# A decode step of cached attention: V of a unit in one load into a buffer of its own, K in three buffers

## The chip, the cores and the metric

The kernel runs on one core of one Trainium2 chip. The metric is the device time of one execution in microseconds, the median of three runs. The span that a profile shows goes from the first to the last instruction of one profiled execution, and is a little shorter than that execution's own time.

## The reference

Two batches with one new token each, width 512. A is attention of 32 query heads over a cache of 8 key/value heads, 32768 positions and a head width of 128; B is a small gated network on the same normalised input. The output is `x + A * silu(B)`.

```python
x = A_x                                    # [2, 1, 512]
xn = _layernorm(x, axis=-1)
# A: q = xn @ wq, 32 heads; k, v: [2, 8, 32768, 128], 4 query heads share one
scores = einsum("bhqd,bhkd->bhqk", q, k) * (128 ** -0.5)
p = softmax(scores)
s = einsum("bhqk,bhkd->bhqd", p, v).reshape(2, 1, 4096) @ wo
# B: h = gelu(layernorm(xn) @ w1), shifted by one or two tokens, @ w2; with one
#    token every shift leaves zeros, so x1 = xn
h2 = gelu(layernorm(x1) @ w3) @ w4
g = silu(x1 + h2)
return x + s * g
```

All tensors are bf16. K and V of the cache have 134 MB each; they are read once, and with the weights 280.5 MB come from HBM.

## The kernel before, in words

The attention is cut into 16 **units**, one for each batch and key/value head (`units`, `NU` = 16). A unit has 8 MB of K and 8 MB of V. Before the change both come in two **chunks** (`NCH` = 2) of 4 MB: a chunk lies in SBUF as 128 partitions with 32 KB each, and is read from HBM as 128 contiguous rows of 32 KB.

A chunk of K is worked on by `k_job`: DVE transposes it in four blocks (`transposed`, one instruction for 2048 words of 4 bytes per partition, into one of `KTB` = 2 buffers `ktb`), and PE makes scores from each block with 8 matmuls (`scores`, into the PSUM tile `sc`). `waiting` is a list of blocks whose scores are still to be issued; `flush(keep)` issues those beyond `keep`, and PE so runs one block behind DVE. When the last scores of a unit are issued, `softmax_front` has DVE take a maximum; the rest of the softmax is two pieces of work (`step1`, `step2`) that are put on the list `glue` and issued one at a time between other work. They end with `pT`, the transposed probabilities.

A chunk of V is worked on by `v_job`: 32 matmuls of four 32-column strips of PE, with 16 columns of `pT` as weights and 512 columns of V, add to the PSUM tile `acc`. After the second chunk `unit_end` copies `acc` and puts the normalisation on `glue`.

`loads` is the one list of all loads, and also the order in which the jobs are issued: the first chunk of K, wq, the second chunk of K, w3, w4, and then for each unit n, chunk by chunk, K of unit n + 1 and V of unit n; last wo. All loads are DMAs on SP's queue, into one pool of `SLOTS` = 5 buffers with 32 KB per partition (`issue`). Load i + 5 is issued in the program after job i; on the chip its DMA waits on SP until the buffer that it takes has been read. The last chunk of V comes in two halves, and wo in four pieces, so that their matmuls can start as each piece lands.

```python
    for n in range(NU):
        for c in range(NCH):
            if n + 1 < NU:
                loads.append(("K", n + 1, c))
            loads.append(("V", n, c))
```

In `v_job` the scores that still wait (`flush(0)`) are issued after the first four matmuls of a chunk, so the scores of the last K block and the value products alternate on PE. The engines follow the order of the program each by itself; the order is written out by hand.

`mlp_job` (network B) stands where w4 stands in `loads`; `q_job` makes the queries within the first chunk of K; `o_final` and `wo_job` make the output from the 16 units.

In the profile L110 is the DMA of K and V, L116 that of wo, L286 the transposes of K, L234 the scores, L313 the value products, L335 the copy of `acc`, L427 the last products of network B, and L365 those of `wo_job`.

Of the kernel before, what the change touches and what calls it, by code (L numbers as in the profile page):

```python
# [9 lines left out]
BF16 = mybir.dt.bfloat16  # L10
# [4 lines left out]

UT = 128
GT = 16
SLOTS = 5
KTB = 2
KG = 2  # L20
LAG = 1
# [3 lines left out]
def kernel(  # L25
# [14 lines left out]
    nc = tc.nc  # L40

    B, Sq, D = A_x.shape
    _, Hkv, Sk, Dh = A_k_cache.shape
    HD = A_wq.shape[1]
    Hq = HD // Dh
    rep = Hq // Hkv
    Fdim = B_w3.shape[1]
    assert Sq == 1 and B == 2 and Dh == 128 and rep == 4 and D == 512 and Fdim % 128 == 0
    DK = D // 128
    FK = Fdim // 128  # L50
    CH = UT * 128
    NCH = Sk // CH
    NB = UT // GT
    NS = 32 // rep
# [8 lines left out]
    NU = len(units)  # L63

    ctx.enter_context(tc.manual_schedule())
    head = ctx.enter_context(tc.tile_pool(name="head", bufs=1))
    slots = ctx.enter_context(tc.tile_pool(name="slots", bufs=SLOTS))
    pers = ctx.enter_context(tc.tile_pool(name="pers", bufs=1))
    kt_pool = ctx.enter_context(tc.tile_pool(name="ktb", bufs=KTB))
    p_pool = ctx.enter_context(tc.tile_pool(name="prob", bufs=2))  # L70
# [12 lines left out]
    NR = HD // 128  # L83
    wo_v = A_wo.rearrange("(p r) d -> p (r d)", r=NR)

    loads = [("K", 0, 0), ("wq",)]
    loads += [("K", 0, c) for c in range(1, NCH)]
    loads += [("w3",), ("w4",)]
    for n in range(NU):
        for c in range(NCH):  # L90
            if n + 1 < NU:
                loads.append(("K", n + 1, c))
            loads.append(("V", n, c))
    wo_cuts = [0, NR // 2, 3 * NR // 4, NR - 4, NR]
    loads += [("wo",)]
    tiles = {}

    def issue(i):
        if i >= len(loads):
            return  # L100
        what = loads[i]
        t = slots.tile([128, UT * Dh], BF16, tag="slot", name=f"slot_{what[0]}")
        if what[0] in ("K", "V"):
            b, g = units[what[1]]
            c = what[2]
            src = A_k_cache if what[0] == "K" else A_v_cache
            sv = src[b, g, c * CH:(c + 1) * CH, :].rearrange("(p t) d -> p (t d)", p=128)
            w = UT * Dh // 2 if what == ("V", NU - 1, NCH - 1) else UT * Dh
            for w0 in range(0, UT * Dh, w):
                nc.sync.dma_start(out=t[:, w0:w0 + w], in_=sv[:, w0:w0 + w])  # L110
        elif what[0] == "wq":
            nc.sync.dma_start(
                out=t[:, 0:DK * HD].rearrange("p (k f) -> p k f", k=DK), in_=wq_v)
        elif what[0] == "wo":
            for r0, r1 in zip(wo_cuts, wo_cuts[1:]):
                nc.sync.dma_start(out=t[:, r0 * D:r1 * D], in_=wo_v[:, r0 * D:r1 * D])  # L116
        elif what[0] == "w3":
            nc.sync.dma_start(
                out=t[:, 0:DK * Fdim].rearrange("p (k f) -> p k f", k=DK), in_=w3_v)
        else:  # L120
            nc.sync.dma_start(
                out=t[:, 0:FK * D].rearrange("p (f d) -> p f d", f=FK), in_=w4_v)
        tiles[what] = t

    issue(0)
    x_bf = tmp.tile([B, D], BF16, tag="row", name="x_bf")
    nc.scalar.dma_start(out=x_bf[:, :], in_=A_x[:, 0, :])
    x4 = pers.tile([128, 128], BF16)
    nc.gpsimd.memset(x4[:, :], 0.0)
    for b in range(B):  # L130
        nc.scalar.dma_start(out=x4[b:128:32, :], in_=A_x[b, 0, :].rearrange("(j c) -> j c", j=4))
    for i in range(1, SLOTS):
        issue(i)


    ident = head.tile([128, 128], BF16)
# [79 lines left out]
    glue = []  # L216
# [73 lines left out]
    def flush(keep):  # L290
        while len(waiting) > keep:
            scores(*waiting.pop(0))
# [10 lines left out]
            if glue:  # L303
                glue.pop(0)()

    def v_job(n, c):
        vv = tiles[("V", n, c)][:, :].rearrange("p (e i t d) -> p e t i d", i=4, t=GT, d=Dh)
        for e in range(NB // 4):
            half, r0 = (c * NB + e * 4) // NS, (c * NB + e * 4) % NS * rep
            pT = unit_st[n]["pT"]  # L310
            for t in range(GT):
                j = t % 4
                nc.tensor.matmul(  # L313
                    acc[32 * j:32 * j + 16, :].rearrange("p (i d) -> p i d", d=Dh),
                    lhsT=pT[:, half * GT + t, r0:r0 + 16],
                    rhs=vv[:, e, t, :, :],
                    start=(c == 0 and e == 0 and t < 4),
                    stop=(c == NCH - 1 and e == NB // 4 - 1 and t >= GT - 4),
                    tile_position=(0, 32 * j),
                )  # L320
                if e == 0 and t == 3:
                    flush(0)
                elif t % 4 == 3 and glue and n == NU - 1:
                    glue.pop(0)()
        if c == NCH - 1:
            unit_end(n)

    s_ps = s_psp.tile([128, 128], F32)
    nc.vector.memset(s_ps[:, :], 0.0)
# [1 line left out]
    def unit_end(n):  # L331
        b, g = units[n]
        st = unit_st.pop(n)
        acs = tmp.tile([128, 4 * Dh], F32, tag="row", name="acs")
        nc.vector.tensor_copy(out=acs[:, :], in_=acc[:, :])  # L335

        def step1():
            ot = mi_psp.tile([128, 2 * rep], F32, tag="mi", name="ot")
            nc.tensor.matmul(ot[:, rep:2 * rep], lhsT=ones_f[:, :], rhs=st["Sm"][:, :], start=True, stop=True)  # L339
            for i in range(4):  # L340
                nc.tensor.matmul(  # L341
                    ot[:, 0:rep], lhsT=acs[:, i * Dh:(i + 1) * Dh], rhs=sel[:, i, :],
                    start=(i == 0), stop=(i == 3))
            rc = sm_pool.tile([128, rep], F32, tag="rc", name="rc")
            nc.vector.reciprocal(out=rc[:, :], in_=ot[:, rep:2 * rep])  # L345
            nc.vector.tensor_tensor(
                out=oQ[:, b, g * rep:(g + 1) * rep], in0=ot[:, 0:rep], in1=rc[:, :], op=ALU.mult)

        glue.append(step1)
# [49 lines left out]
                out=qz[32 * i:32 * i + 32, n % 2, :, c0:c0 + rep], in_=qp[32 * i:32 * i + 32, :, b, g, :])  # L399

    def mlp_job():
        w3 = tiles[("w3",)][:, 0:DK * Fdim].rearrange("p (k q f) -> p k f q", k=DK, f=FK)
        w4 = tiles[("w4",)][:, 0:FK * D].rearrange("p (f d) -> p f d", f=FK)
        hT_ps = mi_psp.tile([128, FK * B], F32, tag="mi", name="hT")
        for f in range(FK):
            for k in range(DK):
                nc.tensor.matmul(  # L407
                    hT_ps[:, f * B:(f + 1) * B],
                    lhsT=w3[:, k, f, :],
                    rhs=xT[:, DK + k, :],  # L410
                    start=(k == 0), stop=(k == DK - 1),
                )
        hf = pers.tile([128, FK * B], F32)
        nc.vector.tensor_copy(out=hf[:, :], in_=hT_ps[:, :])
        x2 = pers.tile([128, FK * B], F32)
        nc.vector.tensor_mul(out=x2[:, :], in0=hf[:, :], in1=hf[:, :])
        nc.vector.tensor_scalar(out=x2[:, :], in0=x2[:, :], scalar1=0.044715, scalar2=1.0, op0=ALU.mult, op1=ALU.add)
        inner = pers.tile([128, FK * B], F32)
        nc.vector.tensor_mul(out=inner[:, :], in0=hf[:, :], in1=x2[:, :])
        th = pers.tile([128, FK * B], F32)  # L420
        nc.scalar.activation(out=th[:, :], in_=inner[:, :], func=ACT.Tanh, scale=GELU_C)
        nc.vector.tensor_scalar(out=th[:, :], in0=th[:, :], scalar1=0.5, scalar2=0.5, op0=ALU.mult, op1=ALU.add)
        h_bf = pers.tile([128, FK * B], BF16)
        nc.vector.tensor_mul(out=h_bf[:, :], in0=hf[:, :], in1=th[:, :])  # L424
        h2_ps = mi_psp.tile([B, D], F32, tag="mi", name="h2")
        for f in range(FK):
            nc.tensor.matmul(  # L427
                h2_ps[0:B, :],
                lhsT=h_bf[:, f * B:(f + 1) * B],
                rhs=w4[:, f, :],  # L430
                start=(f == 0), stop=(f == FK - 1),
            )
        t_f = tmp.tile([B, D], F32, tag="row", name="t_f")
        nc.vector.tensor_add(out=t_f[:, :], in0=xn[:, :], in1=h2_ps[0:B, :])
        sig = tmp.tile([B, D], F32, tag="row", name="sig")
        nc.scalar.activation(out=sig[:, :], in_=t_f[:, :], func=ACT.Sigmoid)
        nc.vector.tensor_mul(out=g_sb[:, :], in0=t_f[:, :], in1=sig[:, :])
        for b in range(B):
            nc.scalar.dma_start(
                out=g4[b:128:32, :], in_=g_sb[b:b + 1, :].rearrange("b (j c) -> b j c", j=4))  # L440


    for i, what in enumerate(loads):
        if what[0] == "K":
            k_job(what[1], what[2])
        elif what[0] == "V":
            if what[2] == 0:
                while glue and unit_st[what[1]]["pT"] is None:
                    glue.pop(0)()
            v_job(what[1], what[2])  # L450
        elif what == ("w4",):
            mlp_job()
        elif what[0] == "wo":
            while glue:
                glue.pop(0)()
            o_final()
            wo_job()
        issue(i + SLOTS)

    sg = tmp.tile([128, 128], F32, tag="row", name="sg")  # L460
    nc.vector.tensor_tensor(out=sg[:, :], in0=s_ps[:, :], in1=g4[:, :], op=ALU.mult)
# [34 lines left out]
```

## Time and profile before

| | |
|---|---|
| median of 3 runs | 660.98 us (660.77 to 661.1) |
| the profiled execution | 660.7 us, its span 658.9 us |
| mean granted TensorE clock | 0.818 |
| busy: PE, weight loads, DVE, ACT | 420.9, 173.8, 365.4, 38.5 us |
| DMA | 280.88 MB, mean 426 GB/s over the span |
| one transpose of K (L286, 128 of them) | 2298 ns |
| K loads (32 of 4096 KB): issue to landing | 39.9 us, median |
| V loads (31 of 4096 KB): issue to landing | 34.3 us, median |

Instructions are told by line, engine, operation and tile; "x28" says that 28 of them are merged. A time in brackets is how long the engine stood idle before, and what ended that. A DMA's line on SPq tells when it was issued, not when its bytes moved. In slices a digit is the busy share in tenths. In stretches each engine has its busy time and number of instructions, and the last three columns are the granted clock of TensorE, the busy share of the 16 DMA engines and GB/s; a DMA packet is booked at one point of time, so that a very short stretch can show a share over 1.

### The profile page before, as it was taken

The page shows a single profiled execution, that of the slowest core. Times are in us where ns is not written, and L with a number is a line of the kernel's source. Part 1 is how long each engine was busy: PE and PEld are TensorE (multiplying, and loading weights), DVE is VectorE, ACT ScalarE, POOL GpSimd, SP SyncE. Part 2 cuts the span into 40 slices and gives each one's busy share as a digit, 9 for nine tenths or more (in the row PEclk, how much of TensorE's full clock was granted, in tenths as well). Part 3 has the DMA queues.
Part 4 walks back from the last instruction along what each step waited for, and adds up shares of the span by engine and source line. Part 5 has one row for each costly group of instructions (what it writes and reads, how often), then busy time and mean ns, then how long its engine had stood idle before and what let it go on. Part 6 is the DMA issues. An engine that isn't in the chain of part 4 may idle for free.

```text
span 658.9 us, 5935 instructions
## 1 busy us (share of the span) xinstructions
PE 420.9 (64%) x2595; PEld 173.8 (26%) x2595; DVE 365.4 (55%) x312; ACT 38.5 (6%) x104; POOL 2.2 (0%) x10
## 2 busy tenths in 40 slices
PE   0587767477575657746567784657668565764775
PEld 0342223132221223222122332223222222322233
DVE  6174856556654645655555654555565455465531
ACT  1103010000000000000000000000000100000000
POOL 1000000000000000000000000000000000000000
PEclk9997877987786898777898686888868688887776
DMA  9999999999999999999999999999999999999995
GB/s 382 420 438 441 417 444 433 426 443 420 442 431 430 439 426 437 432 427 442 427 436 429 430 443 424 437 432 430 443 422 437 432 431 438 425 436 437 430 425 246
DMA packets 10445, 280.88 MB, mean 426 GB/s; under 512 B 1194, under 2 KB 1204, under 8 KB 1460
## 3 DMA queue, kind: packets, MB, share of 16 engines
q1 hardware_dynamic: 10376, 280.50, 98.8%
q8 instruction: 20, 0.33, 0.2%
q14 instruction: 5, 0.04, 0.0%
q10 hardware_dynamic: 44, 0.01, 0.0%
HBM read 280.50 MB, written 0.00 MB: 426 GB/s over the span
## 4 chain that ended last, share of the span: by engine, by line
DMA 71%; PE 17%; DVE 9%; issue 1%; ACT 1%; SPq 0%; DVEq 0%; ACTq 0%
DMA slot_K<-in_A_k_cache_dram 62%; PE sc L234 12%; DVE ktb L286 7%; DMA slot_wo<-in_A_wo_dram 6%; DMA slot_wq<-in_A_wq_dram 3%; PE acc L313 3%; DVE pT L275 1%; ACT pr L271 1%; PE h L427 1%; PE qT L374 1%; PE hT L407 1%; PE bc L264 0%; DVE nb L268 0%; ACT qz L398 0%; DVE Sm L278 0%
## 5 line engine op out<-in xcount | busy, mean ns | idle before, releaser
L234 PE MATMUL sc<-ktb,qz 128*128 128x512 bf16 x1024 | 310.9, 460 | 198.4 <-DVE ktb L286 196.7
L286 DVE STREAM_TRANSPOSE ktb<-slot_K 128x2048 uint32<-128x2048 uint32 x128 | 292.1, 2298 | 169.9 <-DMA slot_K<-in_A_k_cache_dram 142.3
L234 PEld LDWEIGHTS <-qz 128*128 128x128 bf16 x1024 | 110.7, 112 | 369.0 <-issue 305.6
L313 PE MATMUL acc<-slot_V,pT 128*16 128x512 bf16 x1024 | 70.8, 399 | 5.4 <-DMA slot_V<-in_A_v_cache_dram 5.4
L313 PEld LDWEIGHTS <-pT 128*16 128x16 bf16 x1024 | 23.2, 90 | 54.9 <-issue 34.6
L248 DVE TENSOR_REDUCE m<-sc 128x1 f32<-128x1024 f32 x16 | 19.5, 1221 | 29.8 <-PE sc L234 29.8
L398 ACT COPY qz<-qp 32x16 bf16<-32x16 bf16 x64 | 12.9, 201 | 330.0 <-PE sc L234 308.3
L275 DVE STREAM_TRANSPOSE pT<-pr 128x1024 bf16<-128x1024 bf16 x16 | 19.9, 1245 | 21.2 <-ACT pr L271 21.2
L271 ACT ACTIVATE pr<-sc,nb 128x1024 bf16<-128x1024 f32 x16 | 17.8, 1113 | 234.1 <-DVE nb L268 234.1
L335 DVE COPY acs<-acc 128x512 f32<-128x512 f32 x16 | 11.1, 692 | 14.1 <-PE acc L313 14.1
L341 PE MATMUL ot<-sel,acs 128*128 128x4 f32 x128 | 18.2, 265 | 0.3 <-DVE acs L335 0.3
L341 PEld LDWEIGHTS ot<-sel,acs 128*128 128x128 f32 x128 | 17.2, 209 | 0.4 <-DVE acs L335 0.4
L268 DVE TENSOR_SCALAR nb<-bc 128x1 f32<-128x1 f32 x16 | 2.5, 158 | 22.4 <-PE bc L264 22.4
L374 PE MATMUL qT<-xT,slot_wq 128*128 128x2 bf16 x128 | 3.6, 165 | 12.1 <-DMA slot_wq<-in_A_wq_dram 12.1
L264 PEld LDWEIGHTS bc<-ones_f,gx 1*128 1x128 f32 x32 | 6.5, 250 | 12.9 <-issue 10.9
L264 PE MATMUL bc<-ones_f,gx 1*128 1x1 f32 x32 | 7.8, 311 | 1.0 <-DVE gx L258 1.0
L339 PEld LDWEIGHTS ot<-Sm,ones_f 128*128 128x128 f32 x32 | 6.2, 203 | 3.8 <-issue 1.7
L253 PE MATMUL mT<-identf,m 128*1 128x128 f32 x16 | 4.4, 276 | 3.6 <-DVE m L248 3.6
L374 PEld LDWEIGHTS <-slot_wq 128*128 128x128 bf16 x128 | 3.5, 104 | 12.2 <-DMA slot_wq<-in_A_wq_dram 12.2
L427 PE MATMUL h<-slot_w,h_bf 128*2 128x512 bf16 x14 | 4.9, 525 | 1.6 <-DVE h_bf L424 1.6
L345 DVE RECIPROCAL rc<-ot 128x4 f32<-128x4 f32 x16 | 2.4, 149 | 5.5 <-PE ot L341 5.5
L200 PE MATMUL treg<-ident,xn_bf 2*128 2x2 bf16 x4 | 0.3, 174 | 7.8 <-DVE xn_bf L188 7.8
(70 smaller groups left out, 62.4 us busy)
## 6 DMA issues: line engine op xcount, KB each, us to landing
slot_K<-in_A_k_cache_dram SPq DMA_DIRECT2D x32, 4096.0 KB, 39.9
slot_V<-in_A_v_cache_dram SPq DMA_DIRECT2D x31, 4096.0 KB, 34.3
slot_wq<-in_A_wq_dram SPq DMA_DIRECT2D x1, 4096.0 KB, 21.4
slot_V<-in_A_v_cache_dram SPq DMA_DIRECT2D x2, 2048.0 KB, 29.5
slot_w<-in_B_w_dram SPq DMA_DIRECT2D x2, 1792.0 KB, 39.0
slot_wo<-in_A_wo_dram SPq DMA_DIRECT2D x1, 2048.0 KB
slot_wo<-in_A_wo_dram SPq DMA_DIRECT2D x1, 1024.0 KB
slot_wo<-in_A_wo_dram SPq DMA_DIRECT2D x2, 512.0 KB, 38.7
```

The lines of the kernel that those rows point to most:

```text
L234: nc.tensor.matmul(sc[:, half, :].rearrange("p (t k) -> p t k", k=32), lhsT=qz[:, n % 2, k, off:off + 128], rhs=kv[:, k // 2, k % 2, :, :] ...
L248: nc.vector.tensor_reduce(out=m1[:, :], in_=st["sc"][:, :, :].rearrange("p x k -> p (x k)"), axis=AX.X, op=ALU.max)
L264: nc.tensor.matmul(bc[:, :], lhsT=st["gx"][:, :, :].rearrange("o x h -> o (x h)"), rhs=ones_f[0:1, 0:1], start=True, stop=True)
L271: nc.scalar.activation(out=pr[:, :], in_=st["sc"][:, :, :].rearrange("p x k -> p (x k)"), func=ACT.Exp, bias=nb[:, 0:1], scale=inv_sqrt_dh ...
L275: nc.vector.transpose(out=pT[:, :, :].rearrange("p t r -> p (t r)"), in_=pr[:, :])
L286: nc.vector.transpose(out=ktb[:, :], in_=kw)
L313: nc.tensor.matmul(acc[32 * j:32 * j + 16, :].rearrange("p (i d) -> p i d", d=Dh), lhsT=pT[:, half * GT + t, r0:r0 + 16], rhs=vv[:, e, t, ...
L335: nc.vector.tensor_copy(out=acs[:, :], in_=acc[:, :])
L341: nc.tensor.matmul(ot[:, 0:rep], lhsT=acs[:, i * Dh:(i + 1) * Dh], rhs=sel[:, i, :], start=(i == 0), stop=(i == 3))
L374: nc.tensor.matmul(qT_ps[:, h * B:(h + 1) * B], lhsT=w[:, k * HD + h * Dh:k * HD + (h + 1) * Dh], rhs=xT[:, k, :], start=(k == 0), stop=(k ...
L398: nc.scalar.copy(out=qz[32 * i:32 * i + 32, n % 2, :, c0:c0 + rep], in_=qp[32 * i:32 * i + 32, :, b, g, :])
L427: nc.tensor.matmul(h2_ps[0:B, :], lhsT=h_bf[:, f * B:(f + 1) * B], rhs=w4[:, f, :], start=(f == 0), stop=(f == FK - 1),)
```

## The change

K and V no longer share buffers. K keeps chunks of 4 MB and has a pool of `KSLOTS` = 3 buffers with 32 KB per partition; wo takes one of them at the end. V has one buffer with 64 KB per partition (`vslot`), and a unit's V is loaded into it by one DMA of 8 MB. Only the last unit's V is cut into three pieces, of 4, 2 and 2 MB. At the start this buffer holds wq, w3 and w4 side by side.

A partition now holds 64 KB that lie together in HBM, for K as for V. Rows of a V load are so 64 KB long. Rows of a K load keep 32 KB, and lie 64 KB apart.

In the order of loads and jobs both chunks of K of unit n + 1 come before V of unit n. Ahead of V's job all waiting scores and everything on `glue` are issued, and then the 64 value products of the unit in one go. A load is now issued in the program once the job has been issued that frees its buffer (`ready`, `issue_ready`), still in the order of the list.

```diff
-SLOTS = 5
+KSLOTS = 3
...
-    slots = ctx.enter_context(tc.tile_pool(name="slots", bufs=SLOTS))
+    slots = ctx.enter_context(tc.tile_pool(name="slots", bufs=KSLOTS))
+    vslot = ctx.enter_context(tc.tile_pool(name="vslot", bufs=1))
...
+    W3, W4 = DK * HD, DK * HD + DK * Fdim
     loads = [("K", 0, 0), ("wq",)]
     loads += [("K", 0, c) for c in range(1, NCH)]
     loads += [("w3",), ("w4",)]
     for n in range(NU):
-        for c in range(NCH):
-            if n + 1 < NU:
-                loads.append(("K", n + 1, c))
-            loads.append(("V", n, c))
+        if n + 1 < NU:
+            loads += [("K", n + 1, c) for c in range(NCH)]
+        loads.append(("V", n))
...
+    kload = [w for w in loads if w[0] in ("K", "wo")]
+    done = set()
+
+    def ready(what):
+        if what[0] in ("K", "wo"):
+            j = kload.index(what)
+            return j < KSLOTS or kload[j - KSLOTS] in done
+        if what[0] == "V":
+            return ("V", what[1] - 1) in done if what[1] else ("w4",) in done
+        return True
+
+    def issue_ready():
+        while loads and ready(loads[0]):
+            issue(loads.pop(0))
+
+    def issue(what):
+        if what[0] in ("K", "wo"):
+            t = slots.tile([128, UT * Dh], BF16, tag="slot", name=f"slot_{what[0]}")
+        elif what[0] in ("wq", "V"):
+            t = vslot.tile([128, NCH * UT * Dh], BF16, tag="v", name=f"slot_{what[0]}")
+        else:
+            t = tiles[("wq",)]
...
-            sv = src[b, g, c * CH:(c + 1) * CH, :].rearrange("(p t) d -> p (t d)", p=128)
-            w = UT * Dh // 2 if what == ("V", NU - 1, NCH - 1) else UT * Dh
-            for w0 in range(0, UT * Dh, w):
-                nc.sync.dma_start(out=t[:, w0:w0 + w], in_=sv[:, w0:w0 + w])
+            sv = src[b, g, :, :].rearrange("(p t) d -> p (t d)", p=128)
+            if what[0] == "K":
+                nc.sync.dma_start(out=t[:, :], in_=sv[:, what[2] * UT * Dh:(what[2] + 1) * UT * Dh])
+            else:
+                cuts = [0, NCH * UT * Dh]
+                if what[1] == NU - 1:
+                    cuts = [0, UT * Dh, UT * Dh * 3 // 2, NCH * UT * Dh]
+                for w0, w1 in zip(cuts, cuts[1:]):
+                    nc.sync.dma_start(out=t[:, w0:w1], in_=sv[:, w0:w1])
...
-    def v_job(n, c):
-        vv = tiles[("V", n, c)][:, :].rearrange("p (e i t d) -> p e t i d", i=4, t=GT, d=Dh)
-        for e in range(NB // 4):
-            half, r0 = (c * NB + e * 4) // NS, (c * NB + e * 4) % NS * rep
+    def v_job(n):
+        vv = tiles[("V", n)][:, :].rearrange("p (x i t d) -> p x t i d", i=4, t=GT, d=Dh)
+        nx = NCH * NB // 4
+        for x in range(nx):
+            half, r0 = x * 4 // NS, x * 4 % NS * rep
...
-                if e == 0 and t == 3:
-                    flush(0)
-                elif t % 4 == 3 and glue and n == NU - 1:
-                    glue.pop(0)()
-        if c == NCH - 1:
-            unit_end(n)
+        unit_end(n)
...
-    for i, what in enumerate(loads):
+    for what in order:
         if what[0] == "K":
             k_job(what[1], what[2])
         elif what[0] == "V":
-            if what[2] == 0:
-                while glue and unit_st[what[1]]["pT"] is None:
-                    glue.pop(0)()
-            v_job(what[1], what[2])
+            flush(0)
+            while glue:
+                glue.pop(0)()
+            v_job(what[1])
...
-        issue(i + SLOTS)
+        done.add(what)
+        issue_ready()
```

More of the change, by code (lines that the diff above doesn't have):

```diff
@@ L96 @@
     tiles = {}
[L98 to L102, printed above, removed]
+    kload = [w for w in loads if w[0] in ("K", "wo")]
[17 more added lines that the diff above has]
+            t = tiles[("wq",)]
         if what[0] in ("K", "V"):
             b, g = units[what[1]]
-            c = what[2]
             src = A_k_cache if what[0] == "K" else A_v_cache
-            sv = src[b, g, c * CH:(c + 1) * CH, :].rearrange("(p t) d -> p (t d)", p=128)
-            w = UT * Dh // 2 if what == ("V", NU - 1, NCH - 1) else UT * Dh
-            for w0 in range(0, UT * Dh, w):
-                nc.sync.dma_start(out=t[:, w0:w0 + w], in_=sv[:, w0:w0 + w])
+            sv = src[b, g, :, :].rearrange("(p t) d -> p (t d)", p=128)
[7 more added lines that the diff above has]
+                    nc.sync.dma_start(out=t[:, w0:w1], in_=sv[:, w0:w1])
         elif what[0] == "wq":
@@ L118, in issue @@
             nc.sync.dma_start(
-                out=t[:, 0:DK * Fdim].rearrange("p (k f) -> p k f", k=DK), in_=w3_v)
+                out=t[:, W3:W3 + DK * Fdim].rearrange("p (k f) -> p k f", k=DK), in_=w3_v)
         else:
             nc.sync.dma_start(
-                out=t[:, 0:FK * D].rearrange("p (f d) -> p f d", f=FK), in_=w4_v)
+                out=t[:, W4:W4 + FK * D].rearrange("p (f d) -> p f d", f=FK), in_=w4_v)
         tiles[what] = t
-    issue(0)
+    order = list(loads)
+    issue(loads.pop(0))
     x_bf = tmp.tile([B, D], BF16, tag="row", name="x_bf")
@@ L131 @@
         nc.scalar.dma_start(out=x4[b:128:32, :], in_=A_x[b, 0, :].rearrange("(j c) -> j c", j=4))
-    for i in range(1, SLOTS):
-        issue(i)
+    issue_ready()
     ident = head.tile([128, 128], BF16)
@@ L315, in v_job @@
                     lhsT=pT[:, half * GT + t, r0:r0 + 16],
-                    rhs=vv[:, e, t, :, :],
-                    start=(c == 0 and e == 0 and t < 4),
-                    stop=(c == NCH - 1 and e == NB // 4 - 1 and t >= GT - 4),
+                    rhs=vv[:, x, t, :, :],
+                    start=(x == 0 and t < 4), stop=(x == nx - 1 and t >= GT - 4),
                     tile_position=(0, 32 * j),
                 )
-                if e == 0 and t == 3:
-                    flush(0)
-                elif t % 4 == 3 and glue and n == NU - 1:
-                    glue.pop(0)()
-        if c == NCH - 1:
-            unit_end(n)
+        unit_end(n)
     s_ps = s_psp.tile([128, 128], F32)
@@ L401, in mlp_job @@
     def mlp_job():
-        w3 = tiles[("w3",)][:, 0:DK * Fdim].rearrange("p (k q f) -> p k f q", k=DK, f=FK)
-        w4 = tiles[("w4",)][:, 0:FK * D].rearrange("p (f d) -> p f d", f=FK)
+        w3 = tiles[("w3",)][:, W3:W3 + DK * Fdim].rearrange("p (k q f) -> p k f q", k=DK, f=FK)
+        w4 = tiles[("w4",)][:, W4:W4 + FK * D].rearrange("p (f d) -> p f d", f=FK)
         hT_ps = mi_psp.tile([128, FK * B], F32, tag="mi", name="hT")
@@ L457 @@
             wo_job()
-        issue(i + SLOTS)
+        done.add(what)
+        issue_ready()
     sg = tmp.tile([128, 128], F32, tag="row", name="sg")
```

## The prediction

> **What bounds the kernel now.** I read the page first, by its slices and its queues.
>
> ```profile
> PE   0587767477575657746567784657668565764775
> DVE  6174856556654645655555654555565455465531
> DMA  9999999999999999999999999999999999999995
> q1 hardware_dynamic: 10376, 280.50, 98.8%
> ```
>
> PE and DVE are half to three quarters busy, the DMA engines all the time but for the ends. So the next view is the table of stretches, taken over 12 loads of the middle, over the last V halves, and over the edges of the run:
>
> ```profile
> core 0: us, PE busy (x) PEld busy (x) DVE busy (x) ACT busy (x) POOL busy (x), PEclk, DMA share, GB/s
> 109.38:225.55 116.17, 75.33 (x423) 30.03 (x423) 66.26 (x51) 6.03 (x18) 0.00 (x0) 0.81 1.00 432
> 636.00:648.00 12.00, 9.68 (x77) 4.64 (x69) 1.03 (x3) 0.00 (x0) 0.00 (x0) 0.50 1.01 429
> ...
> 3.40:3.60 0.20, 0.00 (x0) 0.00 (x0) 0.20 (x2) 0.20 (x1) 0.00 (x0) 1.00 0.00 0
> 3.60:3.80 0.20, 0.00 (x0) 0.00 (x0) 0.20 (x2) 0.20 (x1) 0.00 (x0) 1.00 3.07 1311
> 4.80:5.00 0.20, 0.00 (x0) 0.00 (x0) 0.20 (x2) 0.00 (x0) 0.00 (x0) 1.00 2.65 1147
> 654.00:654.50 0.50, 0.32 (x13) 0.13 (x5) 0.00 (x0) 0.00 (x0) 0.00 (x0) 0.50 0.16 66
> 654.50:655.00 0.50, 0.03 (x4) 0.03 (x7) 0.00 (x0) 0.00 (x0) 0.00 (x0) 0.76 0.00 0
> ```
>
> The last three columns count: granted PE clock, DMA share, GB/s. The middle has share 1.00 at 432 GB/s; a 4 MB load passes every 116.17 / 12 = 9.68 us. The kernel is one stream of 280.5 MB that never stops. Its time is the stream's rate, plus the ends, plus every moment in which the queue is empty; before, the middle has none. A gain can only come from a higher rate; a loss comes from a hole. So I looked for what the new order of buffers does to the queue, in the timeline of SP's queue and PE around the end of a unit and the end of the kernel:
>
> ```profile
> 112.25 5.18 PE L234 MATMUL sc<-ktb,qz 128*128 128x512 bf16 x16 [2.91 <-DVE ktb L286]
> 573.86 1.69 PE L313 MATMUL acc<-slot_V,pT 128*16 128x512 bf16 x28
> 575.59 0.33 SPq L110 DMA_DIRECT2D slot_K<-in_A_k_cache_dram  x1
> ...
> 612.71 1.69 PE L313 MATMUL acc<-slot_V,pT 128*16 128x512 bf16 x28
> 614.45 2.07 SPq L116 DMA_DIRECT2D slot_wo<-in_A_wo_dram  x4
> 618.63 8.00 PE L234 MATMUL sc<-ktb,qz 128*128 128x512 bf16 x24 [4.23 <-DVE ktb L286]
> 638.72 4.44 PE L313 MATMUL acc<-slot_V,pT 128*16 128x512 bf16 x40
> 654.97 0.40 PE L365 MATMUL s_ps<-slot_wo,oP 128*2 128x128 bf16 x16 [0.65 <-DMA slot_wo<-in_A_wo_dram]
> ```
>
> A load into a used buffer leaves the moment the last product has read it: 575.55 to 575.59. At 614.45 even a quarter of a buffer (the first piece of wo) leaves only after all 32 products of its old content, so a buffer is given back whole.
>
> **The change part by part.**
>
> *The middle, units 1 to 13.* The stream is now K, K, V (8 MB, 19.4 us). Put 0 where V(n-1) has arrived. Its 64 products last 3.9 to 7.1 us (below), so SP issues V(n) by about 8. K(n+1,0) and K(n+1,1) are already queued, and keep the DMA engines busy to 19.4. V(n)'s wait stands ahead of K(n+2,0) on SP, which is wanted only at 38.7, and whose buffer has been free for long. K(n+2,1) needs the transposes of K(n+1,0), which lands at 9.7 and takes 4 x 2.30 us, some 11 with PE's slow start: 21, wanted at 48.4. V has some 11 us of slack, K more. PE must be free when V lands: K(n,1) lands 19.4 us before it, needs 11 us of transposes, 2 of scores and 6 of softmax (m at 629.23 to pT's end at 635.2). DVE has 8 x 2.30 + about 4.6 = 23 us of work in 38.7. Value products gathered into one run of 64 cost nothing here: the stream covers them. If that cover went, 64 products (about 6 us) would be exposed per unit.
>
> *The head.* wq, w3 and w4 now share the V buffer, so V(0) waits for the MLP's last product, 55.3. Ahead of it are queued 12.6 MB of K and wq, 3.7 of w3 and w4, and K(1,0), K(1,1): 24.6 MB. From 2.5 us at 432 GB/s they last to 59.5. V(0) can move bytes at 55.3 + 1.7 = 57.0: no hole, 2.5 us to spare.
>
> *The tail.* Here the order has no K left: K(15,0), K(15,1), V(14), V(15), wo. V(15) needs the buffer that V(14) is landing in, and wo stands behind V(15) on SP, so the queue is empty from V(14)'s last byte to V(15)'s first. Before, V(15) was queued 20 us ahead. The hole, in order:
> - Last byte to first product: the last records of the load end by 654.5, in the end some 654.4, PE starts at 654.97: 0.6 us.
> - 64 products. Warm: 1.69 / 28 = 60 ns each, 3.9 us. At clock 0.50: 4.44 / 40 = 111 ns, 7.1 us. PE has little to do for some 5 us before V(14) lands, and after such gaps the trace starts slow: the 16 scores at 112.25 are 8 at 0.43 and 8 at 0.23 us (3.4 us slow), the 24 at 618.63 about 12 and 12 (5.3 us slow). 31 products at 111 ns + 33 at 60 is 5.4; 48 and 16 is 6.3. I take 5.9.
> - SP to first byte: the first load is issued at 0.73. Records are booked at a packet's end; bunches end at 3.7 and 4.9, so a 32 KB packet takes 1.2 us and the first began near 2.45: 1.7 us.
>
> Sum 8.2 us, ends 6.2 and 9.4. Nothing hides it: after it 8 MB of V and 4 MB of wo follow at full rate, and the last third of V to the last product is as before (16 products, the finishing steps under wo's last 9.7 us).
>
> *Rows of V, 64 KB in place of 32.* No packet of 64 KB is in the trace. Per busy engine, the middle moves 432 / 16 = 27.0 GB/s with 32 KB rows; 636 to 648, all 16 KB rows, 429 / (16 x 1.01) = 26.5. That makes 1212 and 618 ns a packet, so joining two saves 2 x 618 - 1212 = 24 ns. V's 33 x 128 / 16 = 264 packets per engine become 18 x 128 / 16 = 144: 120 x 24 ns = 2.9 us at most, nothing if the row goes as two packets. The share is rounded to 0.01, as large as the effect, so I take 1.3.
>
> *Rows of K, 32 KB each as before, now 64 KB apart.* A gain is excluded, the packets being the same. The nearest strided rows are those of 636 to 648 (16 KB, 32 KB apart). If all their 2% came from the stride, K's 32 x 9.68 = 310 us would lose 5.7. I take 0, since the packet count explains the same 2%.
>
> One page of the Trainium skill speaks against this part: "DMA: Bandwidth & Descriptors", section "Latency and other measured facts", reports copies losing rate when rows lie a large power of two apart, 207 GB/s at 512 KiB against 214 in full. By that 3% K would lose 10 us as an estimate; the trace shows no pitch near it.
>
> *Fewer loads.* V goes from 33 loads to 18. With the queue full, the 0.33 us of an issue on SP lies beside transfers: 0. The same page, section "Anatomy of one DMA", gives each DMA issued from GpSimd some 2 us of fixed cost, which would make 30 us of gain out of 15 loads; a DMA share of 1.00 across 12 loads shows that none of it is paid here.
>
> The profiled execution took 660.7 us (span 658.9 and 1.8 around it), 0.3 under the median. 660.7 + 8.2 - 1.3 = 667.6; with 0.3, **667.9 us**.
>
> **The rivals.**
> 1. *Forecast: a hole at V(15), middle unchanged.* Own range 661.0 + 6.2 - 2.9 to 661.0 + 9.4: 664.3 to 670.4. Chance 0.70.
> 2. *K's stride costs rate.* Hole plus 2 to 6 us more: 670 to 676. For: never shown at 64 KB. Against: 32 KB contiguous is long. 0.12.
> 3. *The single V buffer starves the queue in every unit,* since K stands behind V's wait on SP. It decides only once V(n) leaves over 19 us after V(n-1) landed, where I count 8. Each us beyond costs 14: 675 and above. 0.05.
> 4. *The hole is smaller,* because V(15)'s first piece waits for the first half of the products only: 0.6 + 2.9 + 1.7 = 5.2, so about 664.9. Against: wo's quarter at 614.45. 0.07.
> 5. *Not slower: 64 KB packets are much cheaper.* Place: V's 120 joined packets per engine. It decides when joining two saves over 68 ns (120 x 68 ns = 8.2 us, V at 444 GB/s); the trace's rows give 24 at most. 657 to 661. 0.06.
>
> A form of "the change doesn't do what it says" is a V row sent as two 32 KB packets: case 1 without the 1.3 us.
>
> **How the numbers follow.** This kernel's measurement can tell about 0.2%, 1.3 us, from no change. Cases 1 to 4 are all slower by more: 0.94. Case 5 I split: faster 0.04, same 0.02. The range goes from case 1's lower end, 664, into case 2's middle, 673: it leaves out case 5, case 3 and about half of case 2, some 0.17.
>
> **What would show it.** A stretch near the end where the DMA share falls to 0 for 7 to 9 us, with 64 products of L313's successor in it, starting at the granted clock 0.50; SP's V load issued at their end; the chain of waits passing through those products. Unit for unit the middle should stay at 38.7 us and share 1.00. A stride cost would show as fewer GB/s at share 1.00 while K passes; larger packets as about 1900 fewer on q1 and more GB/s while V passes. The forecast is wrong if holes appear in the middle, if the rate moves over 1%, or if V(15) leaves before V(14)'s products end.

## The result, and the profile after

The changed kernel takes 668.34 us (median of 5 runs, 667.89 to 669.06), the kernel before 660.91 us in the same comparison. The ratio is 1.0115, with a 95% interval of 1.0100 to 1.0129. The forecast was 667.9 us, in a range of 664 to 673. The profiled execution is the one of 668.34 us, its span 666.6.

From the page of the changed kernel, its slices and the queue of the loads:

```profile
DMA  9999999999999999999999999999999999999397
GB/s 378 426 447 423 431 447 441 407 455 417 457 410 444 434 423 456 404 446 425 453 423 416 448 428 442 419 451 428 427 438 417 434 440 440 432 419 465 139 425 300
q1 hardware_dynamic: 8216, 280.50, 97.6%
```

One slice of the forty is new: the third from the end has a DMA share of 0.3 and 139 GB/s. The others swing more than before, because a packet of 64 KB is booked at one point. q1 has 2160 packets fewer: 1920 rows of V that were joined, and 240 small ones that end 15 loads.

The timeline of the same kernel around that slice, PE and SP's queue:

```profile
625.23 5.53 PE L335 MATMUL acc<-slot_V,pT 128*16 128x512 bf16 x64 [5.49 <-DMA slot_V<-in_A_v_cache_dram]
630.81 1.28 SPq L131 DMA_DIRECT2D slot_V<-in_A_v_cache_dram  x3
632.18 2.01 SPq L137 DMA_DIRECT2D slot_wo<-in_A_wo_dram  x4
642.88 3.52 PE L335 MATMUL acc<-slot_V,pT 128*16 128x512 bf16 x32 [10.27 <-DMA slot_V<-in_A_v_cache_dram]
662.46 0.60 PE L381 MATMUL s_ps<-slot_wo,oP 128*2 128x128 bf16 x16 [0.63 <-DMA slot_wo<-in_A_wo_dram]
```

V(14) lands at 625.2, its 64 products run to 630.77, and V(15) leaves SP 0.04 us later, with wo behind it. PE had been idle for 5.49 us before, and waits 10.27 us more for the first piece of V(15). The chain of work that ended last goes through the 64 products and this issue. The stretches of the same kernel show what that does to the DMA engines (last three columns: granted clock, DMA share, GB/s):

```profile
119.45:625.19 505.74, 324.52 (x1833) 134.29 (x1833) 286.40 (x221) 24.51 (x70) 0.00 (x0) 0.80 1.00 430
622.00:622.50 0.50, 0.00 (x0) 0.00 (x0) 0.50 (x2) 0.00 (x0) 0.00 (x0) 0.80 0.30 131
622.50:625.00 2.50, 0.00 (x0) 0.00 (x0) 0.12 (x2) 0.00 (x0) 0.00 (x0) 0.50 0.00 0
625.00:630.00 5.00, 4.77 (x56) 1.88 (x59) 0.00 (x0) 0.00 (x0) 0.00 (x0) 0.59 0.00 0
630.50:631.50 1.00, 0.58 (x10) 0.30 (x2) 0.69 (x1) 0.00 (x0) 0.00 (x0) 1.00 0.00 0
631.50:632.00 0.50, 0.44 (x4) 0.44 (x4) 0.01 (x1) 0.00 (x0) 0.00 (x0) 1.00 2.08 590
633.50:634.00 0.50, 0.00 (x0) 0.00 (x0) 0.00 (x0) 0.00 (x0) 0.00 (x0) 1.00 2.16 918
```

The middle holds a share of 1.00 from V(1)'s landing to V(14)'s: 505.74 / 13 = 38.90 us a unit, against 466.21 / 12 = 38.85 before (109.38 to 575.59). Between 622.5 and 631.5 no load's data begins to move. The last packet of V(14) is booked at 622.3, and PE wakes at 625.23. A packet of 64 KB lasts 2.42 us (median of the trace's packet records), and a record of 4 bytes, with which each DMA engine ends its share of a load, stands at 624.7. So a packet is booked at its start, and the slowest engine stopped at 624.7.

### The profile page after: what moved, and what is told of

The parts are those of the page before. It is cut to its first block, busy times and chain, and to the rows that moved or that the text cites. A ratio compares the mean times of both kernels' runs of the same rounds, so it can differ in the third digit from the quotient of the medians.

```text
span 666.6 us, 5903 instructions
## 1 busy us (share of the span) xinstructions
PE 416.2 (62%) x2595; PEld 178.0 (27%) x2595; DVE 364.1 (55%) x312; ACT 38.5 (6%) x104; POOL 2.4 (0%) x10
## 4 chain that ended last, share of the span: by engine, by line
DMA 73%; PE 14%; issue 1%; DVE 1%; SPq 0%; DVEq 0%
DMA slot_V<-in_A_v_cache_dram 69%; PE acc L335 13%; DMA slot_wo<-in_A_wo_dram 4%; PE sc L255 1%; DVE ktb L307 1%; SPq L137 0%; DVE m L269 0%; SPq L131 0%; PE s_ps L381 0%; PE bc L285 0%; DVE sg L478 0%; DVE out_bf L480 0%; DVE gm L276 0%; PE mT L274 0%; DVE gx L279 0%
## 5 line engine op out<-in xcount | busy, mean ns | idle before, releaser
L255 PE MATMUL sc<-ktb,qz 128*128 128x512 bf16 x1024 | 273.8, 417 | 96.0 <-DVE rc L361 61.6
L307 DVE STREAM_TRANSPOSE ktb<-slot_K 128x2048 uint32<-128x2048 uint32 x128 | 287.0, 2286 | 70.2 <-DMA slot_K<-in_A_k_cache_dram 45.0
L255 PEld LDWEIGHTS <-qz 128*128 128x128 bf16 x1024 | 104.6, 103 | 258.1 <-issue 168.3
L335 PE MATMUL acc<-slot_V,pT 128*16 128x512 bf16 x1024 | 91.3, 533 | 84.9 <-DMA slot_V<-in_A_v_cache_dram 84.9
L335 PEld LDWEIGHTS <-pT 128*16 128x16 bf16 x1024 | 33.4, 116 | 135.7 <-issue 128.1
L285 PE MATMUL bc<-ones_f,gx 1*128 1x1 f32 x32 | 6.3, 265 | 9.3 <-DVE gx L279 9.3
L390 PE MATMUL qT<-xT,slot_wq 128*128 128x2 bf16 x128 | 3.6, 165 | 12.2 <-DMA slot_wq<-in_A_wq_dram 12.2
L285 PEld LDWEIGHTS bc<-ones_f,gx 1*128 1x128 f32 x32 | 5.0, 193 | 13.0 <-DVE gx L279 12.1
L276 DVE TENSOR_REDUCE gm<-mT 1x4 f32<-1x128 f32 x16 | 4.4, 278 | 5.8 <-PE mT L274 5.8
L443 PE MATMUL h<-slot_wq,h_bf 128*2 128x512 bf16 x14 | 6.0, 616 | 1.6 <-DVE h_bf L440 1.6
```

The source lines that it names most:

```text
L255: nc.tensor.matmul(sc[:, half, :].rearrange("p (t k) -> p t k", k=32), lhsT=qz[:, n % 2, k, off:off + 128], rhs=kv[:, k // 2, k % 2, :, :] ...
L285: nc.tensor.matmul(bc[:, :], lhsT=st["gx"][:, :, :].rearrange("o x h -> o (x h)"), rhs=ones_f[0:1, 0:1], start=True, stop=True)
L307: nc.vector.transpose(out=ktb[:, :], in_=kw)
L335: nc.tensor.matmul(acc[32 * j:32 * j + 16, :].rearrange("p (i d) -> p i d", d=Dh), lhsT=pT[:, half * GT + t, r0:r0 + 16], rhs=vv[:, x, t, ...
L390: nc.tensor.matmul(qT_ps[:, h * B:(h + 1) * B], lhsT=w[:, k * HD + h * Dh:k * HD + (h + 1) * Dh], rhs=xT[:, k, :], start=(k == 0), stop=(k ...
L443: nc.tensor.matmul(h2_ps[0:B, :], lhsT=h_bf[:, f * B:(f + 1) * B], rhs=w4[:, f, :], start=(f == 0), stop=(f == FK - 1),)
```

## The experiments

Each was timed in up to 11 runs beside the kernel before, whose median was 660.96 us beside the first four and 661.02 beside the last four. Theory: the added time is one hole, between V(14) and V(15). Rivals: the stride of K, a queue that starves in every unit, the order K, K, V itself.

**1. The last unit's V into the K buffers** (`e1_last_v_elsewhere`). The order K, K, V stays.

```diff
-        loads.append(("V", n))
+        loads += [("V", n)] if n < NU - 1 else [("V", n, 0), ("V", n, 1)]
-    kload = [w for w in loads if w[0] in ("K", "wo")]
+    kload = [w for w in loads if w[0] in ("K", "wo") or len(w) == 3]
...
-        if what[0] in ("K", "wo"):
+        if what in kload:
             t = slots.tile([128, UT * Dh], BF16, tag="slot", name=f"slot_{what[0]}")
...
```

What is left out here splits the load and the products of the last unit between the two buffers.

> The last unit's V goes in two loads of 4 MB into the K buffers that are free by then, so it is queued behind V(14) without waiting for V(14)'s products; all else as in the changed kernel. Theory (the added time is the hole at V(15), with the middle unchanged but for some 1 us that larger packets save): the DMA share has no stretch at 0 near the end, and the time falls from 668.3 by 7 to 8.5 us, to 660 to 661 us, ratio to before 0.998 to 1.001. Rival (the stride of K or a starved queue costs the time): it stays at 665 us or more. Rival (the hole costs 8 us or more and large packets give it back): 659 us or less.

Measured: 660.23 us, ratio to before 0.9989 (0.9980 to 0.9997). The page's slices, then the timeline:

```profile
DMA  9999999999999999999999999999999999999995
...
606.75 0.80 SPq L133 DMA_DIRECT2D slot_V<-in_A_v_cache_dram  x2
615.52 1.75 SPq L139 DMA_DIRECT2D slot_wo<-in_A_wo_dram  x4
625.17 5.66 PE L342 MATMUL acc<-slot_V,pT 128*16 128x512 bf16 x64 [5.15 <-DMA slot_V<-in_A_v_cache_dram]
634.87 2.38 PE L342 MATMUL acc<-slot_V,pT 128*16 128x512 bf16 x32 [2.18 <-DMA slot_V<-in_A_v_cache_dram]
```

V(15)'s pieces and wo leave SP before V(14) has landed; the share never falls. V(14) lands at the same 625.2 as in the changed kernel, and its products are as slow, but nothing waits for them: the first half of V(15) is there at 634.87, where the changed kernel has it at 642.88. The hole is worth 668.34 - 660.23 = 8.1 us, and everything else in the change, the order K, K, V too, is worth a gain of 0.7 us (0.2 to 1.3 by the interval). This version is that much faster than the kernel before.

**2. The products of unit 14 twice** (`e2_products_of_14_twice`), and **3. those of units 0 to 13 twice** (`e3_products_of_0_to_13_twice`). One line, with `n == NU - 2` or `n < NU - 2`:

```diff
-        for x in range(nx):
+        for x in [x for _ in range(2 if n == NU - 2 else 1) for x in range(nx)]:
```

> The 64 value products of unit 14 run twice (the second pass starts the sum anew, so the output is the same). Theory: they lie on the path, in the hole; 64 more at 60 ns, by then at full clock, add 3.8 us: 672.1 us, and V(15)'s load leaves 3.8 us later. Rival (the time is lost elsewhere, V(15) waits for something other than these products): 668.3 us, no change.

> The value products of units 0 to 13 run twice, those of 14 and 15 once (output the same). Theory (V's buffer is free some 11 us before the queue needs it, so 3.8 us more per unit are covered): no change, 668.3 us within 0.7. Rival (the single buffer already starves the queue in each unit): up to 14 x 3.8 = 53 us more; for each us of slack that is missing 14 us.

Measured: 673.68 us (672.15 to 674.07) and 670.10 us (669.88 to 670.42). Timeline of the first:

```profile
625.07 9.70 PE L335 MATMUL acc<-slot_V,pT 128*16 128x512 bf16 x128 [5.13 <-DMA slot_V<-in_A_v_cache_dram]
634.82 1.28 SPq L131 DMA_DIRECT2D slot_V<-in_A_v_cache_dram  x3
667.71 0.60 PE L381 MATMUL s_ps<-slot_wo,oP 128*2 128x128 bf16 x16 [0.61 <-DMA slot_wo<-in_A_wo_dram]
```

The products last 9.70 - 5.53 = 4.2 us longer, and V(15) leaves 4.0 us later: they are on the path, as expected, at 65 ns each in place of 60. The time rose by 5.3 us, not 3.8. The other 1.2 lie behind the hole: from V(15)'s issue to the last piece of wo it is 32.89 us, against 31.65. In the packet records one DMA engine ends wo 1.2 us after the other fifteen; what held it up is told below. One of the five runs, at 672.15, lies 1.4 below the next.

Timeline of the second:

```profile
586.52 8.87 PE L335 MATMUL acc<-slot_V,pT 128*16 128x512 bf16 x128 [3.98 <-DMA slot_V<-in_A_v_cache_dram]
595.45 0.33 SPq L131 DMA_DIRECT2D slot_V<-in_A_v_cache_dram  x1
626.43 5.94 PE L335 MATMUL acc<-slot_V,pT 128*16 128x512 bf16 x64 [4.65 <-DMA slot_V<-in_A_v_cache_dram]
632.42 1.28 SPq L131 DMA_DIRECT2D slot_V<-in_A_v_cache_dram  x3
```

14 x 64 = 896 more products, 54 us of PE's time at 60 ns each, gave 1.8 us. So the middle covers nearly all of them, and the rival of a starved queue falls. The 1.8 us missed the expectation of 0.7 all the same: V(14) landed 1.2 us later than in the changed kernel (626.43 against 625.23) and its products took 0.4 longer. V(13) still landed within 0.3 us. In the packet records one DMA engine ends V(14) at 625.9, the other fifteen by 624.8; this too is told below.

**4. V in two loads into the same buffer** (`e4_v_in_two_loads`).

```diff
-                cuts = [0, NCH * UT * Dh]
+                cuts = [0, UT * Dh, NCH * UT * Dh]
```

> Each unit's V comes in two loads of 4 MB with rows of 32 KB, into the same single buffer. Theory by the packet records of the changed kernel (64 KB in 2418 ns against 2 x 1213): 120 more packets per engine at 8 ns, 1 us more: 669.3 us. By the prediction's upper price, 24 ns: 671.2 us. Rival (larger packets give nothing): 668.3 us.

Measured: 666.44 us (666.27 to 666.75), 1.9 us less than the changed kernel: a miss, and of the wrong sign. The timeline says why:

```profile
620.48 1.90 PE L335 MATMUL acc<-slot_V,pT 128*16 128x512 bf16 x32
625.82 2.81 PE L335 MATMUL acc<-slot_V,pT 128*16 128x512 bf16 x32 [3.44 <-DMA slot_V<-in_A_v_cache_dram]
628.67 1.28 SPq L131 DMA_DIRECT2D slot_V<-in_A_v_cache_dram  x3
```

With two loads, PE multiplies the first half while the second still lands; in the hole stand 32 products, not 64, 2.81 us in place of 5.53. The expectation had priced only the packets. V(14) lands 0.6 us later here (625.82), V(15) leaves 2.1 us earlier. A buffer is given back whole, but it is read piece by piece, as its loads arrive.

**5. Rows 64 KB apart, in the kernel before** (`e5_before_rows_64k_apart`).

```diff
-            sv = src[b, g, c * CH:(c + 1) * CH, :].rearrange("(p t) d -> p (t d)", p=128)
+            sv = src[b, g, :, :].rearrange("(p t) d -> p (t d)", p=128)[:, c * UT * Dh:(c + 1) * UT * Dh]
```

> The kernel before with one change: a partition holds 64 KB that lie together in HBM, so every K and V row of 32 KB lies 64 KB from the next, in K and in V. Theory (the stride costs nothing): 661.0 us, ratio 0.999 to 1.001. Rival (the stride costs rate): up to 2% of the 620 us of K and V, 673 us; by a 3% loss 680 us.

Measured: 660.87 us, ratio 0.9998 (0.9990 to 1.0007). The stretch that was shown for the middle of the kernel before, longer, in this run:

```profile
109.38:575.59 466.21, 302.13 (x1692) 120.61 (x1692) 264.83 (x204) 24.12 (x72) 0.00 (x0) 0.81 1.00 432
```

The same 432 GB/s. The stride costs nothing that can be measured, with K and V both strided.

**6. V in two buffers of 32 KB** (`e6_v_in_two_buffers`).

```diff
-            t = vslot.tile([128, NCH * UT * Dh], BF16, tag="v", name=f"slot_{what[0]}")
+            t = vslot.tile([128, UT * Dh], BF16, tag="va", name=f"slot_{what[0]}")
...
+                t2 = vslot.tile([128, UT * Dh], BF16, tag="vb", name="slot_V2")
...
-                    rhs=vv[:, x, t, :, :],
+                    rhs=vvs[x * 2 // nx][:, x % (nx // 2), t, :, :],
...
```

> The changed kernel with V's one buffer of 64 KB cut into two of 32 KB, each with its own load of 4 MB and given back by itself; w3 and w4 lie in the second. Theory (the hole comes from giving the buffer back as a whole): the first half of V(14) is multiplied while the second lands, so V(15)'s first load leaves before V(14) has landed and the hole is gone; packets are 32 KB again, so 661 us, ratio to before 0.999 to 1.0015. Rival (K ahead of V in the list is what costs): 666 us or more.

Measured: 662.77 us (660.75 to 663.10), ratio 1.0020 (1.0011 to 1.0029): 5.6 us of the 7.4 are gone, and 1.8 are left in the median; two of the ten runs, at 660.75 and 660.99, are as fast as the kernel before. Timeline of the run at 662.93:

```profile
620.73 3.28 PE L338 MATMUL acc<-slot_V,pT 128*16 128x512 bf16 x32
624.06 0.33 SPq L131 DMA_DIRECT2D slot_V<-in_A_v_cache_dram  x1
625.76 1.90 PE L338 MATMUL acc<-slot_V,pT 128*16 128x512 bf16 x32 [1.74 <-DMA slot_V<-in_A_v_cache_dram]
```

The first half of V(14) had landed by 615.7 (packet records); its products stand behind the softmax of unit 15 in PE's order, start after it, and end at 624.01. V(15)'s first load leaves 1.7 us before V(14)'s second half wakes PE, and its first bytes come too late for most DMA engines: in the packet records fourteen of them end V(14) between 620.8 and 624.0 and two at 625.3, and the first packets of V(15) begin from 625.0 to 626.2. So the fourteen are idle for 1.1 us at least and 5.4 at most. The expectation had not priced the softmax ahead of the first half.

**7. Two K buffers in place of three** (`e7_two_k_buffers`): `KSLOTS = 2`.

> The changed kernel with two K buffers in place of three. Theory (the middle has slack: K(n+2,0) can leave some 21 us after V(n-1) landed and is wanted at 38.7, K(n+2,1) at 31 and is wanted at 48.4): no change, 668.3 us within 1.3. Rival (the K loads are what keeps the queue full): holes in each unit, 14 us more for each us that is missing, 680 us or more.

Measured: 668.04 us (667.78 to 669.75), 0.3 under the changed kernel. The K loads have slack, as the prediction counted; the third buffer buys nothing here.

**8. PE kept busy while it waits for V(14)** (`e8_pe_kept_busy`).

```diff
+WARM = 18
...
+            if what[1] == NU - 2:
+                warm = mi_psp.tile([128, 4, 128], F32, tag="mi", name="warm")
+                for _ in range(WARM):
+                    nc.tensor.matmul(
+                        warm[:, :, :], lhsT=qz[:, 0, 0, 0:128], rhs=qz[:, 0, :, 0:128],
+                        start=True, stop=True)
             v_job(what[1])
```

> The changed kernel with 18 extra matmuls of 512 columns, whose result nobody reads, on PE between the softmax of unit 15 and the value products of unit 14, that is in the time in which PE waits for V(14). Theory (PE starts those products at half its clock because it was idle): the 64 products take 3.9 us instead of 5.6, the hole shrinks by 1.7 and the time to 666.6 us. Rival (the products are slow for another reason, such as the fresh load): 5.6 us again and 668.3 us.

Measured: 666.17 us (four runs from 666.08 to 666.25, one at 668.51). Timeline:

```profile
620.05 4.06 PE L470 MATMUL warm<-qz 128*128 128x512 bf16 x18
625.20 3.63 PE L336 MATMUL acc<-slot_V,pT 128*16 128x512 bf16 x64 [1.08 <-DMA slot_V<-in_A_v_cache_dram]
628.87 1.28 SPq L132 DMA_DIRECT2D slot_V<-in_A_v_cache_dram  x3
660.44 0.40 PE L382 MATMUL s_ps<-slot_wo,oP 128*2 128x128 bf16 x16 [0.64 <-DMA slot_wo<-in_A_wo_dram]
```

V(14) lands at the same moment, its 64 products take 3.63 us in place of 5.53, and V(15) leaves 1.9 us earlier; the last products are 0.2 us quicker too. Together that is the 2.2 us by which the time fell. Work that nobody needs made the kernel faster, because it stood before a stretch of PE work that the DMA queue waited for. The Trainium skill, "TensorE: Matmul & The Clock Gate", section "Part 1: The HAM clock gate", says that PE runs at half its clock after idling and at the full one after about 3.4 us of activity; the traces agree: in the changed kernel the granted clock is 0.50 from 625.2 to 629.0 and 0.96 from there to 630.8, in this run 1.00 from 625.2 to 628.8.

## Why the prediction was right

**The mechanism** was the forecast's: the middle kept its rate (38.90 against 38.85 us a unit), and the only new stretch without load data stands between V(14) and V(15). Experiment 1 takes it away and gives back 8.1 us; 2 and 8 lengthen and shorten it, and the time follows.

**The terms of the hole.** Last byte to first product, forecast 0.6: some 0.5 (near 624.7 to 625.23). The 64 products, forecast 5.9: 5.53. The start of the load, forecast 1.7 from SP to the stream: V(15) leaves at 630.81, and its first packets begin at 631.8 to 632.5 but last up to 2.1 us; the second ones begin from 633.5 to 634.0, which at 1.21 us a packet is as if the stream had begun at 632.3 to 632.8, 1.4 to 2.0 after the issue. The sum is 7.5 to 8.1, where 8.2 was forecast and experiment 1 has 8.1.

**The larger packets,** forecast 1.3 out of 0 to 2.9: a joined pair takes 2418 ns against 2 x 1213, 8 ns saved, so 120 x 8 = 1.0 us; experiment 1's gain over the kernel before is 0.7. The gain shows in the middle, too, where no hole blurs it: by the packet records the 225 MB from the 30th MB to the 255th took 520.3 to 520.4 us in the changed kernel and experiments 1, 2, 7 and 8, and 520.8 to 520.9 in the kernel before and in 4, 5 and 6, which have rows of 32 KB. (The units above don't show it, since a landing is as late as its slowest DMA engine.) The upper price of 24 ns was three times too high; it rested on a share that was rounded to 0.01, as was said.

**What was read wrong.** The prediction took records to be booked at a packet's end. They are booked at its start, as V(14)'s last packet shows. The first load's bunch at 3.7 us was thus the second packets and not the first; those begin from 1.76 us. Taking one packet time off that bunch gave the right delay for a wrong reason, by luck: the first packets of an empty queue last longer, here up to 2.1 us in place of 1.21. And the first piece of wo is not a quarter of a buffer but half of one (2 MB); that it had to wait for all 32 products says the same of the buffer.

**The rivals.** K's stride: experiment 5, nothing. The starved queue: experiment 3, 1.8 us where 53 stood to be lost, and experiment 7. A buffer given back by halves: not so with one load (64 products before V(15)), and experiment 6 shows the price when it is made so. Much cheaper packets: 8 ns, not 68. The order K, K, V: experiment 1 keeps it and has lost nothing.

**The engine that comes late.** In experiments 2 and 3 a single DMA engine adds 1.2 us. The packet records show what came between. Besides the loads (q1) the pages list a queue q8; here it is in the changed kernel and in experiment 3:

```profile
q8 instruction: 20, 0.33, 0.2%
q8 instruction: 27, 0.44, 0.2%
```

A q8 packet has 16 KB and takes 0.9 us. The load packet that begins as it ends takes 0.5 us longer than the others of its size, for all 18 q8 packets ahead of the hole in the changed kernel. So the engines drift apart in steps of about 1.3 us: seven end V(14) at 620.3 to 621.1, seven at 623.1 to 623.5, two at 624.4 and 624.7. In experiment 3, whose PE has 896 more matmuls, 25 q8 packets pass in the same time; seven engines end at 620.3 to 620.9, one at 623.1, seven at 624.5 to 624.8, and one at 625.9. In experiment 2, with 64 more matmuls and 21 q8 packets, one packet falls at 660.9 into wo, where none does in the changed kernel (630.1, in the hole, and 661.7, as wo ends): for its 0.9 us one engine moves no load data, and one engine ends wo 1.2 us late. This is read from the records; no experiment changed q8 alone.

The slowest engine sets each landing. In the hole the engines were idle for 7.0 us at least and 12.2 at most, and after it all end wo within 661.5 to 662.1; before, without a hole, they ended from 650.2 to 654.6.

**What stays open:** why single runs of experiments 2, 6, 7 and 8 lie 1.1 to 2.4 us from the others; only one run of each has a profile.

## What to carry to other kernels

When the DMA queue is the bound, ask of each buffer whether something is still queued behind the load that waits for it. A single large buffer can be safe for the whole run, because other loads cover its turnover, and still cost one full turnover at the end of the list, where the cover runs out; there, let the last load borrow a buffer that nobody needs any more. And whatever runs in such a gap counts with its cold price: PE that waited for data starts slowly (5.53 us for the 64 products here, 3.63 when it was kept busy).

## What the runs showed of the hardware

A V row of 64 KB goes as one packet, 2418 ns, and one of 32 KB takes 1213: from 32 to 64 KB there is next to nothing left to gain. Rows of 32 KB can lie 64 KB apart without loss (ratio 0.9998, 0.9990 to 1.0007); the Trainium skill, "DMA: Bandwidth & Descriptors", section "Latency and other measured facts", which reports a loss at 512 KiB, is not contradicted at a pitch that it doesn't list. The 16 DMA engines ended V(14) up to 4.4 us apart (620.3 to 624.7) after 500 us at a share of 1.00, and the steps between them go with the 16 KB packets of queue q8, some 1.3 us each.
